# Two MLPs behind retention attention: layer 2's first product of two groups as seven half-depth products, with the decay mask made on the chip, eight more load buffers and idle matmuls at the start

## The chip, the cores and the metric

The kernel runs on one core of a Trainium2 chip. The metric is the device time of one execution in microseconds (us); shown is the median of three runs. Engines: TensorE (PE) multiplies matrices, VectorE (DVE), ScalarE (ACT) and GpSimd (POOL) work on elements, SyncE (SP) issues the DMAs, which run on the core's DMA engines.

## What is computed

Retention attention over 2 batches, 8 heads, 768 steps, head width 64; its output, as 1536 tokens of width 512, goes through two MLPs of hidden width 2048. Everything is float32.

```python
gamma = 1.0 - 2.0 ** (-5.0 - np.arange(H, dtype=np.float32))
for t in range(S):
    state = gamma[None, :, None, None] * state + np.einsum('bhd,bhe->bhde', k[:, :, t], v[:, :, t])
    y[:, :, t] = scale * np.einsum('bhd,bhde->bhe', q[:, :, t], state)
...
h = x @ w_in                      # layer 1
P = a[0] + a[1] * h + a[2] * h2 + a[3] * h3
Q = 1.0 + np.abs(b[0]) * np.abs(h) + np.abs(b[1]) * h2
x = (P / (Q + 1e-06)) @ w_out
...
h = x @ w_in                      # layer 2
y = (h * (1.0 / (1.0 + np.exp(-h)))) @ w_out
```

## The kernel before

The attention is cut into 12 chunks of 128 tokens. A chunk loads q and k transposed (`qT`, `kT`) and k and v (`kn`, `vn`), makes scores on PE (L435), multiplies them by the decay mask `msk` on DVE (`am`, L317), forms the output from the masked scores and v (L480) and from the state (L490), and grows the state (L468), which DVE keeps in `bd`. Four chunks make a group of 512 tokens; there are three groups, 0, 1 and 2.

Each MLP product is made of three matmuls on split operands: high part times high part, low times high, high times low. High parts of x lie in `xh[g]`, low ones in `xl[g]`, those of the weights in slots (`ih`, `il` for the first product, `oh`, `ol` for the second). The hidden width is cut into 16 blocks of 128, two to a pair. A step is one group and one block: 12 matmuls of 128x512 into one of the banks `h0` and `h1` (`mm_in`, L526), the activation on ACT and DVE, the split of the result into `gh` (ACT) and `gl` (DVE or POOL), and 12 matmuls into the four banks `acc0` to `acc3` (L576). A layer is 3 groups x 8 pairs x 2 steps. In layer 1 the runs of pairs are mixed between the groups so that the MLP can begin when group 0 has its four chunks; in layer 2 the groups come in the order 1, 0, 2.

Weights: `weights()` loads 512 KB in two halves per pair, converts them on ACT and DVE into `wt`, splits them on ACT (high, L386) and on POOL or DVE (low, L391), and stores `wt` to DRAM (`spill`), from where later groups load it again. There are four slots, and two more once the attention's buffers are free.

Helpers record every operation: `act` (L309), `tt` (L317), `stt` (L324), `dma` (L343, DMAs on SP). The order of all operations on all engines is one table, `ORDER`, read by `Flow.order`; the numbers in `R` are those with which the table was planned. At the start eleven idle matmuls (L644) run on PE while the first loads come in, and the mask `msk` is loaded from DRAM (512 KB).

Of the kernel before, what the change touches and what calls it, by code (L numbers as in the profile page):

```python
# [23 lines left out]
R = {'lw': -463.92, 'T0': 689.59, 'tau0': 13.93, 'tau1': 122.19, 'c0': -129.63, 'dc': 67.51, 'conv': 39.61, 'half': 427.29, 'absl': -34.77, 'raw': 455.03, 'ret': 752.06, 'spl': -417.39, 'hi': 301.24, 'lo': 31.56, 'inn': -277.93, 'later': -32.81, 'split': -554.53, 'out': 359.39, 'evac': -363.13, 'qload': -20.08, 'scl': 238.79, 'sc': 858.37, 'am': -44.15, 'gr': 112.48, 'av': -547.62, 'bd': 198.47, 'xh': -201.14, 'xl': 110.32, 'glp': 25, 'lop1': 15, 'lop2': 30, 'scp': 0, 'ps': 17, 'ksc': 103.89, 'qa': -467.29, 'ka': 4, 'late': 20, 'mid': 4, 'pev': -317.29, 'pld': -385.01, 'cg': -489.85, 'wm': 11, 'mk': 26.43, 'ck': 21.3, 'g2': (1, 0, 2), 'ch0': 269.21, 'ch1': -102.81, 'ch2': 64.3, 'ch3': 22.33, 'ch4': -52.46, 'ch5': 5.42, 'ch6': -78.23, 'ch7': 237.84, 'ch8': 90.06, 'ch9': -61.88, 'ch10': -106.39, 'ch11': -212.52, 'ru0': 218.22, 'lu0': -107.8, 'ru1': 40.68, 'lu1': -106.06, 'ru2': 91.09, 'lu2': 146.01, 'ru3': -37.17, 'lu3': -39.51, 'rhalf': 125.38}  # L24
# [11 lines left out]
    '3f9Kq7zc;LI4FTNa6Ha{=}-YHVJVD;@o*Gm!z`E`lVNg9fmtyJ=ENb85>sJntb-%5F6P3aFbD=iZp?%AurW5pCO86X;zXQ)qoF>Ig)z_!Ti_^c',
    'iIZ?NPR5xq4W{E#n2*b#F*U&PkOsSAcbo`QU;?DabeI-1U|wvF-LMso#nw0#C&6Tx3caug_Qp1t4{PB#oQC;vHWb1FSP<J{J6w)EaR&CmzSs{J',
    ';!IqC?Xf=&z*)EgS7JjPh;v{r%*Hji2v^}+oCh6n5H`YDuoHLTZd{G~a1ZXsb+{fk;6~hpi*YYDp{8^I58@&0gq?8#bj0~E1iRo|yo`tO2sWeU',
    'v=E-+Qd|s6;3{s$qj&`u!415IH*p1Qf{ic-r{HqvNUNb0^`J4h0k+_CT!!;-4IIN~cpW>@EqsNmU?sf97ucC@;~l(<ZKxLw!=X4Bx8V-lil=Zb',
    '9LJZ~noi>z>`8C2E#1TKxE=3fJL*mE@I8LO_H+V&;yU<&E$Ab5p{~@2e&HYdi|gSxKERgr2}4q73Ps^43|+v7corYwXWR@YaS5Km#k7hx(mw=3',  # L40
# [696 lines left out]
```

## Time and profile before

| | |
|---|---|
| median of three runs | 593.6 us (593.54 to 593.75) |
| the profiled execution's own time | 591.33 us |
| its span, from first to last instruction | 589.5 us |
| mean granted clock of PE | 0.997 |
| PE, DVE, ACT, POOL busy | 574.0, 417.5, 394.2, 132.9 us |

Busy time is the sum over an engine's instructions, share of the span in brackets in the rows below. The granted clock is a share of PE's full speed. A name such as `h` in the trace stands for all buffers of that name (`h0` and `h1`). The trace records a float32 matmul of the attention and of the warming twice, one of the MLP products once.

### The profile page before, as it was taken

Reading aid. Unit: us, or ns where it says so; the run is one execution under the profiler, and the core shown is the slowest. Engines: PE = TensorE matmul, PEld = TensorE weight load, DVE = VectorE, ACT = ScalarE, POOL = GpSimd, SP = SyncE. Lnnn points to the kernel's source line nnn. Section 1 sums busy time; section 2 is a strip of 40 time slices with the busy share of each in tenths; the row PEclk is TensorE's granted clock in tenths of the full one; section 3 lists DMA queues with packets and bytes.
Section 4 is the critical chain, followed back from the end, with each engine's and each line's share of the span. In section 5 each row is a group of like instructions: output and inputs, shape, how many; then the busy total and the mean of one; then the engine's idle time right before and its main releaser. Section 6 shows DMA issues by size and latency. Waiting matters only on the chain.

```text
span 589.5 us, 8100 instructions
## 1 busy us (share of the span) xinstructions
PE 574.0 (97%) x2950; PEld 474.0 (80%) x2950; DVE 417.5 (71%) x646; ACT 394.2 (67%) x690; POOL 132.9 (23%) x104
## 2 busy tenths in 40 slices
PE   6969999999999999999999999999999999999997
PEld 5858787888888888888888888878888888888885
DVE  2899999999899999999999977765332213233320
ACT  7887788999999887787999887764522312424212
POOL 0554674464435200000114364300000000000000
PEclk9998999999999999999999999999999999999999
DMA  8996855543122201302226565462320000130001
GB/s 327 339 370 239 303 192 162 180 125 117 62 81 81 73 1 36 126 18 91 76 68 214 179 212 152 156 217 84 108 89 1 1 1 18 54 123 3 0 1 72
DMA packets 33368, 70.02 MB, mean 119 GB/s; under 512 B 3632, under 2 KB 3632, under 8 KB 33328
## 3 DMA queue, kind: packets, MB, share of 16 engines
q1 hardware_dynamic: 33328, 69.51, 35.1%
q8 instruction: 23, 0.38, 0.3%
q14 instruction: 17, 0.14, 0.1%
HBM read 56.91 MB, written 12.58 MB: 118 GB/s over the span
## 4 chain that ended last, share of the span: by engine, by line
PE 91%; DMA 4%; DVE 2%; ACT 1%; issue 1%; SPq 0%; ACTq 0%
PE acc L576 43%; PE h L526 43%; DMA kT<-in_kt_dram 2%; PE a L490 2%; PE a L435 2%; PE a L480 1%; DVE wt L324 1%; DMA raw<-in_moe_w_out_dram 1%; DMA qT<-in_qt_dram 1%; PE a L468 1%; SPq L343 0%; ACT raw L309 0%; DVE am L317 0%; DVE w L324 0%; PE h L468 0%
## 5 line engine op out<-in xcount | busy, mean ns | idle before, releaser
L526 PE MATMUL h<-xh,ih 128*128 128x512 f32 x384 | 150.2, 391 | 0.1
L526 PE MATMUL h<-xh,il 128*128 128x512 f32 x384 | 149.5, 389 | 0.0
L526 PE MATMUL h<-xl,ih 128*128 128x512 f32 x384 | 149.4, 389 | 0.0
L324 DVE SCALAR_TENSOR_TENSOR w<-w,h 128x512 f32<-128x512 f32 x48 | 32.6, 684 | 78.4 <-ACT w L309 78.2
L526 PEld LDWEIGHTS h<-xh,ih 128*128 128x128 f32 x384 | 72.1, 188 | 16.1 <-DVE s L324 0.6
L526 PEld LDWEIGHTS h<-xh,il 128*128 128x128 f32 x384 | 72.1, 188 | 15.0
L526 PEld LDWEIGHTS h<-xl,ih 128*128 128x128 f32 x384 | 72.1, 188 | 14.8
L309 ACT ACTIVATE w<-h 128x512 f32<-128x512 f32 x48 | 28.1, 593 | 78.7 <-PE h L526 74.2
L576 PE MATMUL acc<-gh,oh 128*128 128x512 f32 x192 | 75.9, 395 | 0.0
L576 PE MATMUL acc<-gh,ol 128*128 128x512 f32 x192 | 74.8, 390 | 0.0
L576 PE MATMUL acc<-gl,oh 128*128 128x512 f32 x192 | 74.8, 390 | 0.0
L576 PE MATMUL acc<-oh,gh 128*128 128x512 f32 x192 | 74.7, 389 | 0.0
L576 PE MATMUL acc<-ol,gh 128*128 128x512 f32 x192 | 74.7, 389 | 0.0
L576 PE MATMUL acc<-oh,gl 128*128 128x512 f32 x192 | 74.7, 389 | 0.0
L317 DVE TENSOR_TENSOR gl<-w,gh 128x512 fp32r<-128x512 f32 x48 | 34.0, 715 | 44.1 <-ACT gh L309 44.1
L391 POOL TENSOR_TENSOR ol<-wt,oh 128x512 fp32r<-128x512 f32 x28 | 38.6, 1389 | 105.6 <-ACT oh L386 94.4
L309 ACT ACTIVATE gh<-w 128x512 fp32r<-128x512 f32 x48 | 29.8, 629 | 46.7 <-PE acc L576 31.6
L324 DVE SCALAR_TENSOR_TENSOR wt<-wt,raw 128x512 int32<-128x512 int32 x64 | 45.0, 707 | 12.0 <-ACT raw L309 7.2
L391 POOL TENSOR_TENSOR il<-wt,ih 128x512 fp32r<-128x512 f32 x28 | 39.5, 1419 | 51.3 <-ACT ih L386 34.2
L309 ACT ACTIVATE raw<-raw,par 128x512 int32<-128x512 uint32 x64 | 48.1, 758 | 1.5 <-DMA raw<-in_moe_w_in_dram 0.8
L324 DVE SCALAR_TENSOR_TENSOR s<-s,par,h 128x512 f32<-128x512 f32 x65 | 48.2, 744 | 1.0
L317 POOL TENSOR_TENSOR gl<-s,gh 128x512 fp32r<-128x512 f32 x26 | 35.2, 1353 | 59.4 <-ACT gh L309 37.7
(88 smaller groups left out, 960.2 us busy)
## 6 DMA issues: line engine op xcount, KB each, us to landing
raw<-in_moe_w_out_dram SPq DMA_DIRECT2D x32, 512.0 KB, 3.7
raw<-in_moe_w_in_dram SPq DMA_DIRECT2D x32, 512.0 KB, 4.6
spill<-wt SPq DMA_DIRECT2D x32, 256.0 KB, 4.6
wt<-spill SPq DMA_DIRECT2D x32, 256.0 KB, 3.0
qT<-in_qt_dram SPq DMA_DIRECT2D x12, 256.0 KB, 5.7
kT<-in_kt_dram SPq DMA_DIRECT2D x12, 256.0 KB, 5.7
vn<-in_v_dram SPq DMA_DIRECT2D x12, 256.0 KB, 6.0
kn<-in_k_dram SPq DMA_DIRECT2D x10, 256.0 KB, 5.6
```

The source lines that it names most:

```text
L309: lambda: nc.scalar.activation(out=out_, in_=in_, func=func, **kw),
L317: op(eng, dur, rank, lambda: e.tensor_tensor(out=out_, in0=in0, in1=in1, op=alu), reads, writes, port)
L324: lambda: nc.vector.scalar_tensor_tensor(out=out_, in0=in0, scalar=scalar, in1=in1, op0=op0, op1=op1),
L391: e.tensor_tensor(out=sl.t[nm + "l"][:, us], in0=wt.t, in1=sl.t[nm + "h"][:, us].bitcast(F32), op=ALU.subtract)
L435: nc.tensor.matmul(heads(sb_[j].t)[:, hp, :], kT.t[js, hp, :], qT.t[js, hp, :], start=True, stop=True)
L468: nc.tensor.matmul(st.t[j * D : (j + 1) * D, hp * D : (hp + 1) * D], kn.t[:, 2 * hp + j, :], vn.t[:, 2 * hp + j, :], start=(hp == 0), stop ...
L480: nc.tensor.matmul(heads(xo.t)[j * D : (j + 1) * D, hp, :], vn.t[:, 2 * hp + j, :], heads(am[j].t)[:, hp, :], start=(hp == 0), stop=not mo ...
L490: nc.tensor.matmul(heads(xo.t)[:, hp, :], old.t[:, hp, :], qT.t[:, hp, :], start=False, stop=True, skip_group_check=True,)
L526: nc.tensor.matmul(h.t, sl.t[w][:, ws], x[g].t[:, c, :], start=(n == 0), stop=(n == 3 * KD - 1))
L576: nc.tensor.matmul(a.t, a1, a2, start=(first and n == 0), stop=(last and n == 2))
```

## The change

In layer 2 the group 1 is worked as before. Then groups 0 (`ga`) and 2 (`gb`) are taken together, pair by pair from 7 down to 0 (`joint`): their first products, two groups by two blocks, are made as seven products of half the depth (L798, 6 matmuls each) of sums of weights and sums of x, and put together by five additions out of PSUM on DVE. The sums of x are made once during the stage of group 1 (`x_sums`, L689, L706) into slots 4 and 5; the sums of weights in each pair, with their high and low parts in the space of `xh[1]` and `xl[1]`. Only group 0's second products (`project`, L628) run in the joint stage; the gates of group 2 go to DRAM (`gates`, 16 of 256 KB) and come back for a last stage, which only makes second products (`remaining`). In layer 2 four slots are left for weights.

At the start the mask is no longer loaded: 256 KB of decays come in, are spread over the partitions by two float32 matmuls (L902) and made into `msk` by eight DVE operations (L912). Eight buffers for `kT` and `vn` of the chunks 2 to 5 are lent from space that is used for weights later; `vn` has two turns in place of three, `qT` four in place of three. Eleven groups of three idle matmuls (L927) stand between the first chunks' work. All scaling of k runs on POOL. The table `ORDER` is another one. Diff, cut to its core:

```diff
-            runs = [(g, range(NPR) if n % 2 == 0 else range(NPR - 1, -1, -1)) for n, g in enumerate(R["g2"])]
+            g1, ga, gb = R["g2"]
+            runs = [(g1, range(NPR)), ((ga, gb), range(NPR - 1, -1, -1)), ((gb,), range(NPR))]
...
+        if l == 1 and use_order[i - 1][0] == 0:
+            free = [r for r in free if r < RING]
+            resident = {key: r for key, r in resident.items() if r < RING}
...
-    again = {key for key, _, old in loads.values() if old}
+    again = {(key, h) for i, (key, _, old) in loads.items() if old for h in range(2) if use_order[i][1] != (gb,) or h}
+    again |= {((1, p), 0) for p in range(NPR)}
...
+    gates = [Buf(f"gate{f}", [P, GT], F32, dram) for f in range(NF)]
...
+    spare = [x for n in ("u2", "s1", "r", "t") for x in ew[n].bufs]
...
-    kns, vns = Turns("kn", 3, [P, H, D], F32, at), Turns("vn", 3, [P, H, D], F32, at)
-    qTs, kTs = Turns("qT", 3, [P, HP, P], F32, at), Turns("kT", 2, [P, HP, P], F32, at)
+    kns, vns = Turns("kn", 3, [P, H, D], F32, at), Turns("vn", 2, [P, H, D], F32, at)
+    qTs, kTs = Turns("qT", 4, [P, HP, P], F32, at), Turns("kT", 2, [P, HP, P], F32, at)
+    first_stack = ExitStack()
+    fpool = first_stack.enter_context(tc.tile_pool(name="first", bufs=1, side="right", reuse_waits="tile"))
+    lent = {
+        (n, c): Buf(f"{n}_c{c}", [P, H, D] if n in ("kn", "vn") else [P, HP, P], F32, fpool) for n, c in R["lent"]
+    }
     gqs = Turns("gq", 2, [P, HP, P], F32, at)
     ams = [Buf(f"am{j}", [P, GT], F32, at) for j in range(2)]
...
+            buf = lent.get((name, c)) or turns()
...
-        op("pe", 2.72, now - R["inn"], mm_in, win + xh[g].all + xl[g].all, [h])
+        op("pe", 2.72, now - R["inn"], mm_in, win + xh[g].all + xl[g].all, [h] + [fill] * (s == 0))
...
+    def sum_part(i, c, lo):
+        sl, n = slots[RING + i // 2], "io"[i % 2] + "hl"[lo]
+        return sl, n, slice(c * GT, (c + 1) * GT), sl.cells[n, c]
...
+        for c in range(2):
+            chain(0, c, (of(xh[gb], c), of(xh[ga], c)), ((*of(xl[gb], c), add), (*of(xl[ga], c), sub)))
+        for c in range(2):
+            t1 = full[0, c]
+            chain(1, c, (of(xh[gb], 2 + c), (lambda t1=t1: t1.t, [t1])), ((*of(xl[gb], 2 + c), add),))
+        for c in range(2):
+            t2 = full[1, c]
+            chain(3, c, (of(xh[ga], 2 + c), (lambda t2=t2: t2.t, [t2])), ((*of(xl[ga], 2 + c), add),))
+        for c in range(2):
+            chain(2, c, (of(xh[gb], 2 + c), of(xh[gb], c)), ((*of(xl[gb], 2 + c), add), (*of(xl[gb], c), sub)))
...
+    def joint(u, p, first, last):
+        now = at_step[2 * u]
+        sl = slots[slot_of_use[u]]
+        q = p % 2
+        wu = []
+        for half in range(2 if u in loads else 1):
+            for un in range(2):
+                wt = wts()
+                kept = spill[(1, p), half, un]
+                dma(now - R["ret"] + half, 0.66, wt.t, kept.t, [kept], [wt])
+                if u in loads:
+                    parted(u, 1, sl, "io"[half], un, wt, now - R["conv"] + R["half"] * half + un)
+                if half == 0:
+                    wu.append(wt)
+        (a11, a21), (a12, a22) = (
+            [wt.t[:].rearrange("p (c j f) -> p j c f", c=2, j=2)[:, j] for j in range(2)] for wt in wu
+        )
+        tmp = [temp(), temp()]
+        s1, s2, s3, s4 = (t.t[:].rearrange("p (s c f) -> p s c f", s=2, c=2)[:, i] for t in tmp for i in range(2))
+        rk = now - R["wsum"]
+        tt("dve", rk, s1, a21, a22, ALU.add, wu, [tmp[0]], n=GT // 2)
+        tt("dve", rk, s2, s1, a11, ALU.subtract, [wu[0]], [tmp[0]], n=GT // 2)
+        tt("dve", rk, s3, a11, a21, ALU.subtract, [wu[0]], [tmp[1]], n=GT // 2)
+        tt("dve", rk, s4, a12, s2, ALU.subtract, [wu[1], tmp[0]], [tmp[1]], n=GT // 2)
+        wh, wl = xh[g1], xl[g1]
+        for r in range(2):
+            k = 2 * q + r
+            act(rk, wh.t[:, k, :], tmp[r].t, AF.Copy, [tmp[r]], wh.cells[k])
+            tt("dve", rk, wl.t[:, k, :], tmp[r].t, wh.t[:, k, :].bitcast(F32), ALU.subtract, [tmp[r], *wh.cells[k]], wl.cells[k])
...
+        def product(b_, w, x, start):
+            def mms():
+                n = 0
+                for c in range(2):
+                    for wlo, xlo in ((0, 0), (0, 1), (1, 0)):
+                        nc.tensor.matmul(
+                            b_.t, w[0](c, wlo), x[0](c, xlo), start=(start and n == 0), stop=(n == 5), skip_group_check=True
+                        )
+                        n += 1
+            op("pe", 1.36, now - R["inn"], mms, w[1] + x[1], [b_])
+        n = NPR - 1 - p
+        b0_, b1_, b2_ = (bank[("a0", "a1", "h0", "h1")[(3 * n + i) % 4]] for i in range(3))
+        c12, c21, c22 = temp(), temp(), temp()
+        def plus(to, b_, x):
+            tt("dve", now, to.t, b_.t, x.t, ALU.add, [b_, x], [to], port=False)
+        product(b0_, block(0, 0), x_of(ga, 0), True)
+        act(now, c12.t, b0_.t, AF.Copy, [b0_], [c12], True)
+        product(b1_, wsum(1), xsum(1), True)
+        plus(c21, b1_, c12)
+        product(b0_, block(1, 0), x_of(ga, 1), False)
+        product(b1_, wsum(0), xsum(0), False)
+        plus(c22, b1_, c12)
+        product(b2_, wsum(2), xsum(2), True)
+        plus(c22, b2_, c22)
+        product(b1_, wsum(3), x_of(gb, 1), False)
+        plus(c12, b1_, c12)
+        product(b2_, block(1, 1), xsum(3), False)
+        plus(c21, b2_, c21)
+        for j, (h, psum_h, mine) in enumerate(((b0_, True, True), (c12, False, False), (c21, False, True), (c22, False, False))):
+            w = ew["w"]()
+            act(now, w.t, h.t, AF.Tanh, [h], [w], psum_h, scale=0.5)
+            to = w if psum_h else h
+            stt(now, to.t, w.t, 1.0, h.t, ALU.add, ALU.mult, [w, h], [to], port=not psum_h)
+            j = j // 2
+            if mine:
+                second(now, ga, sl, j, to, first and j == 0, last and j == 1)
+            else:
+                dma(now + R["spl"], 0.66, gates[2 * p + j].t, to.t, [to], [gates[2 * p + j]])
+    def second(now, g, sl, j, gv_, first, last):
+        gh, gl = ghs(), gls()
+        act(now + R["split"], gh.t, gv_.t, AF.Copy, [gv_], [gh])
+        tt("dve", now + R["split"], gl.t, gv_.t, gh.t.bitcast(F32), ALU.subtract, [gv_, gh], [gl])
+        project(now, 1, g, sl, j, gh, gl, first, last, None)
+    def remaining(u, p, first, last):
+        sl = slots[slot_of_use[u]]
+        for j in range(2):
+            now = at_step[2 * u + j]
+            gv_ = temp()
+            dma(now - R["ret"], 0.66, gv_.t, gates[2 * p + j].t, [gates[2 * p + j]], [gv_])
+            second(now, gb, sl, j, gv_, first and j == 0, last and j == 1)
...
-    warm = ew["u2"].bufs[0]
+    warm = Buf("warm", [P, P])
...
+    shared[1] = gqs()
+    dma(R["mk"], 0.66, shared[1].t[:].rearrange("p a x -> p (a x)"), decays[0], [], [shared[1]])
+    pick, ones = ew["s1"].bufs[0], ew["s1"].bufs[1]
...
+    for j in range(2):
+        b_ = bank[f"acc{2 + j}"]
+        def spread(j=j, b_=b_):
+            nc.tensor.matmul(
+                b_.t, pick.t[:, j * P : (j + 1) * P], shared[1].t[:].rearrange("p a x -> p (a x)"), start=True, stop=True
+            )
+        op("pe", 0.88, R["mk"], spread, [pick, shared[1]], [b_])
+        for a in range(HP):
+            op(
+                "dve",
+                0.27,
+                R["mk"],
+                lambda j=j, a=a, b_=b_: nc.vector.scalar_tensor_tensor(
+                    out=msk.t[:, j, a, :],
+                    in0=heads(b_.t)[:, a, :],
+                    scalar=gk[:, 1, 2 * a + j : 2 * a + j + 1],
+                    in1=ones.t[:, 0:P],
+                    op0=ALU.mult,
+                    op1=ALU.mult,
+                ),
+                [b_, cst, ones],
+                [mcs[j]],
+            )
...
+    def filling():
+        for _ in range(3):
+            nc.tensor.matmul(bank["h0"].t[:, 2 * P : 3 * P], warm.t[:, 0:P], warm.t[:, 0:P], start=True, stop=True)
+    for n in range(R["fill"]):
+        op("pe", 0.65, R["fl"] + 1.5 * n, filling, [warm], [fill])
...
-        if u in loads:
+        if u in loads and g != (ga, gb):
             weights(u)
+        if l == 1 and use_order[u - 1][0] == 0:
+            x_sums(at_step[2 * u + 6])
         opens = u == 0 or use_order[u - 1][:2] != (l, g)
         closes = u == n_use - 1 or use_order[u + 1][:2] != (l, g)
         part = "out" if l == g == 0 and u < NPR else "in" if l == g == 0 else None
+        if g == (ga, gb):
+            joint(u, p, opens, closes)
+            s += 2
+            continue
+        if g == (gb,):
+            remaining(u, p, opens, closes)
+            s += 2
+            continue
         for n, j in enumerate((0, 1) if p % 2 == 0 else (1, 0)):
             step(s, l, g, u, j, opens and n == 0, closes and n == 1, part)
             s += 1
...
```

PE at the very start, before (`a0`, `a1`, `acc0`, `h1` are banks; L435 makes scores, L480 outputs):

```order
L644 MATMUL h1_156<-u2_0_132 128x128 x11
L435 MATMUL a0_149<-qT_0_168,kT_0_171 128x128
L435 MATMUL a1_150<-qT_0_168,kT_0_171 128x128
...
L435 MATMUL acc0_151<-qT_1_169,kT_1_172 128x128
L435 MATMUL acc1_152<-qT_1_169,kT_1_172 128x128
...
L480 MATMUL h1_156<-am0_175,vn_0_165 64x128
L480 MATMUL h1_156<-am1_176,vn_0_165 64x128
```

and now (L867 is the warming, L902 the spreading, L927 idle matmuls, L474 scores):

```order
L867 MATMUL h1_186<-warm_218 128x128 x11
L902 MATMUL acc3_184<-gq_0_214,s1_0_166 128x512
L902 MATMUL acc2_183<-gq_0_214,s1_0_166 128x512
L927 MATMUL h0_185<-warm_218 128x128 x6
L474 MATMUL a0_179<-qT_0_197,kT_0_201 128x128
L474 MATMUL a1_180<-qT_0_197,kT_0_201 128x128
...
L927 MATMUL h0_185<-warm_218 128x128 x6
L474 MATMUL acc2_183<-qT_2_199,kT_c2_206 128x128
L474 MATMUL acc3_184<-qT_2_199,kT_c2_206 128x128
```

Two spreading matmuls and six idle ones stand ahead of the first scores, six more ahead of the second chunk's.

DVE in layer 2 about where the joint stage begins: before, only gates (L324) and their low parts (L317):

```order
L324 SCALAR_TENSOR_TENSOR w_1_135<-w_1_135,h1_156 128x512
L317 TENSOR_TENSOR gl_1_147<-w_0_134,gh_1_144 128x512
L317 TENSOR_TENSOR gl_2_148<-w_1_135,gh_2_145 128x512
L324 SCALAR_TENSOR_TENSOR w_0_134<-w_0_134,h0_155 128x512
L317 TENSOR_TENSOR gl_0_146<-w_0_134,gh_0_143 128x512
```

and now the additions out of the banks `a0`, `a1`, `h0` (L350), weight sums of 256 columns, low parts of sums into `xl1` and `il5`, and gates (L357):

```order
L350 TENSOR_TENSOR xl1_69<-u2_0_162,xh1_68 128x512
L689 TENSOR_TENSOR il5_1683<-t_0_171,ih5_1682 128x512
L350 TENSOR_TENSOR s1_1_167<-a1_180,u2_1_163 128x512
L350 TENSOR_TENSOR u2_0_162<-wt_4_161,wt_0_157 128x256
L350 TENSOR_TENSOR s1_1_167<-h0_185,s1_1_167 128x512
L350 TENSOR_TENSOR t_0_171<-a0_179,r_1_170 128x512
L350 TENSOR_TENSOR u2_0_162<-u2_0_162,wt_4_161 128x256
L350 TENSOR_TENSOR u2_1_163<-a1_180,u2_1_163 128x512
L350 TENSOR_TENSOR xl1_69<-u2_0_162,xh1_68 128x512
L357 SCALAR_TENSOR_TENSOR u2_1_163<-w_1_165,u2_1_163 128x512
L350 TENSOR_TENSOR s1_0_166<-h0_185,s1_0_166 128x512
L350 TENSOR_TENSOR t_1_172<-a0_179,r_1_170 128x512
```

The sums of the next pairs' weights and the additions of the pairs under way share the engine.

SP late in layer 2: before, reloads of weights and stores of the output:

```order
L343 DMA wt_4_131<-spill1601_113 128x512
L343 DMA wt_2_129<-spill1011_107 128x512
L343 DMA wt_3_130<-spill1600_112 128x512
L343 DMA wt_2_129<-spill1700_116 128x512
L621 DMA out_0_dram<-t_0_141 128x512
```

and now, at the end of the joint stage, gates going out and coming back:

```order
L376 DMA wt_1_158<-spill1510_124 128x512
L376 DMA gate2_136<-s1_2_168 128x512
L376 DMA gate1_135<-s1_0_166 128x512
L376 DMA gate0_134<-u2_0_162 128x512
L376 DMA s1_0_166<-gate8_142 128x512
L376 DMA s1_2_168<-gate1_135 128x512
L376 DMA s1_1_167<-gate0_134 128x512
L376 DMA gate3_137<-r_1_170 128x512
L376 DMA wt_3_160<-spill1610_128 128x512
L376 DMA r_0_169<-gate2_136 128x512
```

A gate's load stands right behind the stores of the last gates.

## Rows read from the trace of the kernel before

**Rows 1.** The page, parts 1 and 4: busy time, chain that ended last

```profile
PE 574.0 (97%) x2950; PEld 474.0 (80%) x2950; DVE 417.5 (71%) x646; ACT 394.2 (67%) x690; POOL 132.9 (23%) x104
...
PE 91%; DMA 4%; DVE 2%; ACT 1%; issue 1%; SPq 0%; ACTq 0%
PE acc L576 43%; PE h L526 43%; DMA kT<-in_kt_dram 2%; PE a L490 2%; PE a L435 2%; PE a L480 1%; DVE wt L324 1%; DMA raw<-in_moe_w_out_dram 1%; DMA qT<-in_qt_dram 1%; PE a L468 1%; SPq L343 0%; ACT raw L309 0%; DVE am L317 0%; DVE w L324 0%; PE h L468 0%
```

**Rows 2.** Busy time by stage; columns stand in the first line

```profile
core 0: us, PE busy (x) PEld busy (x) DVE busy (x) ACT busy (x) POOL busy (x), PEclk, DMA share, GB/s
6.48:27.58 21.10, 15.76 (x248) 14.25 (x248) 14.74 (x25) 18.15 (x50) 7.80 (x6) 1.00 1.02 365
...
34.10:47.65 13.55, 9.12 (x113) 7.97 (x113) 12.27 (x20) 10.67 (x18) 8.78 (x7) 0.87 0.97 345
...
126.70:328.00 201.30, 201.30 (x889) 166.26 (x889) 195.63 (x301) 177.47 (x298) 49.13 (x36) 1.00 0.26 83
...
415.00:502.00 87.00, 87.00 (x386) 72.06 (x384) 25.05 (x39) 24.31 (x43) 0.00 (x0) 1.00 0.12 37
502.00:589.50 87.50, 83.35 (x368) 68.72 (x366) 24.80 (x38) 25.86 (x46) 0.00 (x0) 1.00 0.12 43
```

**Rows 3.** The chain in layer 2, from 440: start us, us, what

```profile
439.83 2.72 PE acc L576 x12
442.55 2.72 PE h L526 x12
```

**Rows 4.** Timeline of PE, 0 to 28: start, us, what, idle before, releaser

```profile
1.45 5.03 PE L644 MATMUL h<-u 128*128 128x128 f32 x22 [1.45 <-DVE par L648]
...
21.45 1.16 PE L435 MATMUL a<-qT,kT 64*128 64x128 f32 x16 [0.82 <-DMA qT<-in_qt_dram]
22.54 0.69 PE L468 MATMUL h<-vn,kn 128*64 128x64 f32 x16
23.06 0.28 PE L480 MATMUL h<-u,vn 128*64 128x128 f32 x1
...
24.03 1.16 PE L490 MATMUL h<-qT,bd 128*128 128x128 f32 x8
25.12 0.69 PE L468 MATMUL h<-vn,kn 128*64 128x64 f32 x16
```

**Rows 5.** Timeline of PE, 34 to 48

```profile
36.66 1.09 PE L480 MATMUL a<-am,vn 128*64 128x128 f32 x16 [1.39 <-DVE am L317]
...
41.01 1.16 PE L435 MATMUL a<-qT,kT 64*128 64x128 f32 x16 [1.56 <-DVE bd L317]
43.66 0.98 PE L468 MATMUL a<-vn,kn 128*64 128x64 f32 x16 [1.49 <-DVE am L317]
44.42 1.92 PE L480 MATMUL a<-am,vn 128*64 128x128 f32 x16
46.28 1.62 PE L490 MATMUL a<-qT,bd 128*128 128x128 f32 x8
47.65 0.48 PE L526 MATMUL h<-xh,ih 128*128 128x512 f32 x1
```

**Rows 6.** Timeline of DVE at the start

```profile
9.62 1.29 DVE L317 TENSOR_TENSOR am<-a,msk 128x512 f32<-128x512 f32 x2 [8.21 <-DMA msk<-in_consts_dram]
...
23.37 0.42 DVE L317 TENSOR_TENSOR bd<-h,bd 64x256 f32<-64x256 f32 x1
```

**Rows 7.** Timeline of DVE in layer 2

```profile
440.49 1.29 DVE L324 SCALAR_TENSOR_TENSOR w<-w,h 128x512 f32<-128x512 f32 x2 [3.50 <-ACT w L309]
442.48 0.69 DVE L317 TENSOR_TENSOR gl<-w,gh 128x512 fp32r<-128x512 f32 x1 [0.70 <-ACT gh L309]
```

**Rows 8.** Timeline of ACT in layer 2

```profile
441.81 0.63 ACT L309 ACTIVATE gh<-w 128x512 fp32r<-128x512 f32 x1 [1.35 <-DVE w L324]
```

**Rows 9.** DMA issues from 384 on: KB each, median us to landing

```profile
wt<-spill SPq DMA_DIRECT2D x16, 256.0 KB, 3.3
spill<-wt SPq DMA_DIRECT2D x8, 256.0 KB, 3.6
```

**Rows 10.** A stretch of the start by windows, columns as in rows 2

```profile
43.40:46.80 3.40, 3.14 (x34) 2.81 (x35) 3.36 (x6) 1.85 (x4) 1.98 (x2) 0.57 1.02 386
```

More of the change, by code (lines that the diff above doesn't have):

```diff
@@ L36 @@
[L36 to L40, printed above, removed]
@@ L256, in __init__, with make @@
             self.chunk = [[r[o] for r in self.cells] for o in range(CPG)]
+        def make(self, pool=cpool):
+            self.t = pool.tile([P, KD, GT], F32R, tag=self.name, name=self.name)
     xh = [Parted(f"xh{g}") for g in range(NG)]
     xl = [Parted(f"xl{g}") for g in range(NG)]
+    for g in range(NG - 1):
+        xh[g].make()
+        xl[g].make()
     class Slot:
@@ L352, in weights @@
         for half in range(2):
+            if half == 0 and use_order[u][1] == (gb,):
+                continue
             w = w_dram[l][half].bitcast(I32)
@@ L448, in attention @@
                 ALU.mult,
-                [sb_[j], msk],
+                [sb_[j], mcs[j]],
                 [am[j]],
@@ L455, in attention @@
         if more:
-            gq = shared[ci] if ci in shared else load(0.5, gqs, decays[ci - 1])
-            shared[ci] = gq
+            if ci not in shared:
+                shared[ci] = load(0.5, gqs, decays[ci - 1])
+            gq = shared[ci]
             eng = "dve" if c < R["scp"] else "pool"
@@ L558, in step, with project @@
         tt("pool" if s <= R["glp"] else "dve", now + R["split"], gl.t, gv_.t, gh.t.bitcast(F32), ALU.subtract, [gv_, gh], [gl])
+        project(now, l, g, sl, j, gh, gl, first, last, part)
+    def project(now, l, g, sl, j, gh, gl, first, last, part):
         for m in range(4):
@@ L624, in step, with lazy, rows @@
                 )
-    dma(R["mk"], 1.32, msk.t[:].rearrange("p j a t -> p (j a t)"), consts[:, NGAM:], [], [msk])
+    def lazy(eng, rank, out_, in0, in1, alu, reads, writes, n=GT, port=True):
+        e = {"dve": nc.vector, "pool": nc.gpsimd}[eng]
+        dur = 0.07 + n / 960.0 if eng == "dve" else n / 418.0
+        op(eng, dur, rank, lambda: e.tensor_tensor(out=out_(), in0=in0(), in1=in1(), op=alu), reads, writes, port)
+    def rows(x, k):
+        return lambda: x.t[:, k, :].bitcast(F32)
@@ new lines, in sum_part, with x_sums, split, chain @@
+    def sum_part(i, c, lo):
+        sl, n = slots[RING + i // 2], "io"[i % 2] + "hl"[lo]
+        return sl, n, slice(c * GT, (c + 1) * GT), sl.cells[n, c]
+    def x_sums(rank):
+        sub, add = ALU.subtract, ALU.add
+        full = {}
+        def split(i, c, t):
+            sh_, nh, cs, ch = sum_part(i, c, 0)
+            sl_, nl, cs, cl = sum_part(i, c, 1)
+            op("act", 0.52, rank, lambda: nc.scalar.activation(out=sh_.t[nh][:, cs], in_=t.t, func=AF.Copy), [t], [ch])
+            lazy(
+                "dve", rank, lambda: sl_.t[nl][:, cs], lambda: t.t, lambda: sh_.t[nh][:, cs].bitcast(F32), sub, [t, ch], [cl]
+            )
+        def chain(i, c, first, terms):
+            t = temp()
+            full[i, c] = t
+            (f0, r0), (f1, r1) = first
+            lazy("dve", rank, lambda: t.t, f0, f1, sub, r0 + r1, [t])
+            for f, r, alu in terms:
+                lazy("dve", rank, lambda: t.t, lambda: t.t, f, alu, r, [t])
+            split(i, c, t)
+        def of(x, k):
+            return rows(x, k), x.cells[k]
+        for c in range(2):
[8 more added lines that the diff above has]
+            chain(2, c, (of(xh[gb], 2 + c), of(xh[gb], c)), ((*of(xl[gb], 2 + c), add), (*of(xl[gb], c), sub)))
```

195 lines of the change are left out of this document (131 added, 64 removed).

## The prediction

> **What bounds the kernel now.** I read the page's busy line and its chain first [rows 1]: TensorE (PE) is busy 97% of the span, 91% of the chain that ended last is PE, and the two lines of the MLP products, L526 and L576, hold 43% each. The reader should see that VectorE (DVE, 71%) and ScalarE (ACT, 67%) do not set the total. An average hides stages, so the windows come next [rows 2]: from 126.70 to 328 and from 415 to 502 PE is busy every microsecond (201.30 of 201.30, 87.00 of 87.00). Its only idle time before the tail lies at the start: 21.10 - 15.76 = 5.3 us up to 27.58 and 13.55 - 9.12 = 4.4 us up to 47.65. So a change pays in two ways: by fewer matmuls anywhere, or by filling these early gaps. The chain in layer 2 [rows 3] gives the price of a matmul: twelve of L526 follow each other in 2.72 us, twelve of L576 too, 0.227 us each, with nothing between. Last I read PE's own timeline of the start [rows 4, 5], where each wait stands in brackets with what ended it.
>
> **Term A, the products.** In layer 2 a pair of hidden blocks cost groups 0 and 2 two steps of twelve L526 matmuls each, 48. The change makes seven half-depth products of six matmuls (L798), 42. Six fewer in eight pairs are 48 fewer, of one shape: 48 x 0.227 = **-10.9 us**. The second products (L576, now L628) stay at 384. Because PE has no idle time there [rows 2], this is gained in full unless a new wait takes its place.
>
> **Term B, the start.** Removed: a 512 KB load (msk). In exchange the change loads 256 KB of decays first and spreads them with two fp32 matmuls of 128x512. It lends eight buffers so that chunks 2 to 5 load early, runs chunks 0 to 4 to the end before the first MLP step, and adds 33 idle matmuls in groups of three.
> - A chunk costs on PE: scores 22.54 - 21.45 = 1.09, state growth 0.52, local outputs 0.97, outputs of the state 1.09, together 3.67 us [rows 4]. Five chunks without what chunks at a sequence's head skip: 5 x 1.09 + 5 x 0.97 + 3 x 1.09 + 5 x 0.52 = 16.2.
> - An idle matmul: the trace records every fp32 matmul twice. The eleven of L644 (x22) took 5.03 us, 0.46 each; four of the same shape at L490 took 25.12 - 24.03 = 1.09, 0.27 each with the start of their group [rows 4]. I take 0.23, since they follow others without such a start: 33 x 0.23 = 7.6 us. The ends are 7.1 and 15.1. The two spreading matmuls have four times the columns: about 2.0 together.
> - Walk: the warming ends near 6.2, + 2.0 + 7.6 + 16.2 = 32.0. Two steps of 2.72 end at 37.5. Chunk 5 with its mask wait (3.7 + 1.4, [rows 5]) ends at 42.6. The third step needs bank h0, which DVE should release near 43.0. With chunk 6, which stood ahead of it before (3.7), this point is reached at 46.7, where the kernel before stands at 47.65 [rows 5]: **-0.9 us**. Loads don't hold it: the queues move 365 GB/s [rows 2], 0.72 us per 256 KB, and the last load for chunk 4 is about the 32nd such piece, in by 27.
> - The bounds: -4 if the idle matmuls all lie inside the waits that remain, +3 if they all lie on the path. Of the DVE rows, the mask used to come by DMA and the first masked product waited 8.21 us for it [rows 6]. Eight small multiplications now make it, a 64x256 one costs 0.42 [rows 6], so some 3 us from the spreading on: ready near 11, where it is first asked for near 12. The cover is thin, and if it goes the wait is under 1 us.
>
> **Term C, the joint stage.** Per pair PE runs 42 + 24 matmuls, 66 x 0.227 = 15.0 us. DVE runs four half-width sums, two low halves of them, five additions out of PSUM, four multiplications for the gates and two low halves of gates: 4 x 0.42 [rows 6] + 13 x 0.65 = 10.1 us (two rows of layer 2 together take 1.29, [rows 7]), 12.7 where weights are converted too. ACT runs 9 to 13 of some 0.63 [rows 8], 8 us at most. Neither is the bound by its sum. A product that adds onto a bank must wait for the addition that reads that bank, but the order mostly puts one or two products (1.36 each) or second products between. At the start ten products stand in a row with none of layer 2's second products between, while DVE still has the sums of the pairs 7, 6 and 5 to make: I walked DVE's rows there and find one wait of some **+1.3 us** for the low half of pair 5's weight sums. Bounds: 0, and 3.
>
> **Term D, the gates that go out and come back.** The last gates of group 2 are added, passed through tanh, multiplied, stored (3.6), loaded (3.3, [rows 9]) and split. With 0.6 to 0.7 for each of five steps beside it and the issues' own time, 13.7 us, against 63 matmuls between, 14.3 us. I take **+0.5 us** for the join. The other fourteen have more room. SP's queue gets 62 more rows, but moves 37 to 43 GB/s in these stages [rows 2], a tenth of what it moved at the start. In the first stage of layer 2 DVE gets 36 more sums, some 130 rows in 90 us, 1.4 per us, under the 301 in 201.30 us of layer 1 [rows 2], where PE never waited: 0.
>
> **Sum.** -10.9 - 0.9 + 1.3 + 0.5 = -10.0. The profiled execution took 591.3 us, so 581.3 by its clock. The median of the runs is 593.6, 2.3 above it, and I carry that over: **583.6 us**.
>
> **The clock.** In the stretch from 43.40 to 46.80 the granted clock was 0.57 of full speed [rows 10], close to the lower of the levels 1.2 and 2.4 GHz, after waits of 1.39, 1.56 and 1.49 us [rows 5]; chunk 6's outputs took 1.92 and 1.62 there, [rows 5] where 0.97 and 1.09 are usual [rows 4]. The idle matmuls may keep such a stretch away, and 1.5 us with it, which is part of the bound of -4 in term B. The Trainium skill, "TensorE: Matmul & The Clock Gate", section "Part 1: The HAM clock gate", says that the throttled state is the default and that activity releases it. By that rule these rows are as they should be, and term B would come out nearer to -2.4 than to -0.9.
>
> **Rivals.**
> - A, the start pays in full and the joint stage doesn't wait: -10.9 - 4.0 - 0.5 = -15.4, **578.2 us**. For it: 9.7 us of idle time to fill [rows 2]. Against: PE's work there grows by 9.6 us.
> - B, the start loses: idle matmuls at 0.3 instead of 0.23, or DVE, 12.27 of 13.55 us busy [rows 2], a step behind: **587.5 us** (+3 in place of -0.9).
> - C, **slower**: the joint stage is bound by the round trip product, addition, product. Five additions per pair wait on PE and PE on them. If each is exposed at 0.69 [rows 7], it is 8 x 3.45 = 27.6 us; half of it exposed, 13.8, gives **597.4 us**. It decides from 10.0 / 8 = 1.25 us per pair above my walk. Against: second products stand between after pair 5. For: kernel before never needs such a turn, as its banks h0 and h1 alternate, and a wait for ACT between a product and its gate (3.50, [rows 7]) is hidden only by that.
> - D, PE's short waits in the joint stage pull the clock to its lower level, as they did at 43.40: four such stretches of 3.4 us at 0.57 [rows 10] cost 1.5 each, +6, **589.6 us**. The Trainium skill, same page, section "A second HAM failure mode: psum-queue depth-cycling", tells of just this: short idle times of PE between groups of matmuls that cycle through the banks, and a clock that swings between its levels. No stretch of layer 2 in the trace before shows it, since PE doesn't pause there.
> - E, the change doesn't do what it says: the stored gates return late because their loads stand in SP's queue behind stores that wait for DVE. At 1.2 us for each of the eight last pairs, 9.6: **593.2 us**.
>
> **How the numbers follow.** Forecast 0.53 (its own range 580 to 587), A 0.17, B 0.14, C 0.08, D 0.05, E 0.03. What a measurement of this kernel can tell from no change is about 0.2%, 1.2 us. Faster by more: the forecast, A, B and D, 0.89, less a little for B's and D's upper tails, 0.88. Within: E and the lowest of C, 0.04. Slower: C, 0.08. The range leaves out C, E and a little of A's lower end: 577.5 to 590.0.
>
> **What would show it.** Right: L798 with 336 matmuls of 0.227 apart, and a joint stage that lasts about 8 x 15.0 + 1.3 = 121 us with PE busy 99%; the wait of about 1 us near its start, for DVE's low half (line 350); the third step of L575 near 43; no wait for a gate over 0.5 us. Wrong: a sum of PE's waits in the joint stage above 5 us, for DVE's additions; a granted clock under 1.00 there; the third step later than 46; or a DMA behind PE's wait at the last stage.

## The result and the profile after

The changed kernel takes 586.83 us (median of four, 586.64 to 589.0), the kernel before 593.57 (median of four, 590.82 to 593.75): a ratio of 0.990, 95% interval 0.987 to 0.993, so 6.7 us less. The two profiled executions are nearer to each other: their spans are 584.7 and 589.5, 4.8 us apart. Executions of the kernel before spread with their mean granted clock (in the last comparison below its spans run from 587.7 at a mean clock of 1.000 to 594.3 at 0.987), those of the changed kernel all have 1.000, and the profiled one of before, at 0.997, is among its shorter ones.

The page of the changed kernel, parts 1 and 4, beside [rows 1]:

```profile
PE 575.3 (98%) x2972; PEld 471.9 (81%) x2972; DVE 491.0 (84%) x794; ACT 408.6 (70%) x697; POOL 120.3 (21%) x97
...
PE 79%; DVE 8%; DMA 6%; ACT 4%; issue 2%; SPq 0%; ACTq 0%; DVEq 0%
```

TensorE is busier than before (575.3 against 574.0 us), though 48 matmuls are gone: the idle ones and the two spreading ones took their place. Its share of the chain fell from 91% to 79%, and VectorE and DMAs now hold 14% of it. Its waits in the whole execution (engine, line, what was waited for: us in total, times, longest):

```profile
PE a L520 <- DVE am L350: 1.4, 1, 1.4
PE h L575 <- DVE s L357: 1.2, 1, 1.2
PE h L867 <- DVE warm L863: 1.1, 1, 1.1
PE h L927 <- ACT bd L342: 0.9, 1, 0.9
PE a L508 <- POOL kn L350: 0.4, 1, 0.4
PE acc L628 <- DVE gl L350: 0.2, 1, 0.2
PE h L520 <- DVE xl L557: 0.2, 1, 0.2
```

All but one of them lie before 48 us. The stages, in the columns of [rows 2]:

```profile
0.00:47.65 47.65, 42.41 (x439) 36.09 (x440) 35.04 (x65) 26.95 (x48) 22.91 (x24) 1.00 0.91 314
...
126.70:328.00 201.30, 201.30 (x920) 164.60 (x919) 193.14 (x300) 170.50 (x285) 39.86 (x30) 1.00 0.24 78
...
400.00:526.00 126.00, 125.77 (x552) 103.21 (x551) 102.40 (x180) 59.23 (x107) 0.00 (x0) 1.00 0.31 105
```

The joint stage (400 to 526, with the end of group 1 at its start) is full: 125.77 of 126. The chain inside it:

```profile
441.77 1.36 PE h L798 x6
443.13 1.36 PE a L798 x6
444.49 2.72 PE h L798 x12
447.21 2.04 PE acc L628 x9
```

Six matmuls of L798 in 1.36 us, 0.227 each, back to back with one another and with the second products, as L526 and L576 were [rows 3]. The timeline of TensorE at the start, beside [rows 4, 5]:

```profile
1.12 4.53 PE L867 MATMUL h<-warm 128*128 128x128 f32 x22 [1.12 <-DVE warm L863]
5.48 1.88 PE L902 MATMUL acc<-gq,s 128*128 128x512 f32 x4
7.20 1.50 PE L927 MATMUL h<-warm 128*128 128x128 f32 x12
8.63 1.16 PE L474 MATMUL a<-qT,kT 64*128 64x128 f32 x16
...
13.38 0.94 PE L927 MATMUL h<-warm 128*128 128x128 f32 x6
14.24 0.69 PE L508 MATMUL h<-vn,kn 128*64 128x64 f32 x16
15.85 0.94 PE L927 MATMUL h<-warm 128*128 128x128 f32 x6 [0.93 <-ACT bd L342]
...
34.40 0.50 PE L575 MATMUL h<-xh,ih 128*128 128x512 f32 x1
...
42.62 1.09 PE L520 MATMUL a<-am,vn_c 128*64 128x128 f32 x16 [1.39 <-DVE am L350]
...
45.22 0.69 PE L508 MATMUL a<-vn_c,kn 128*64 128x64 f32 x16 [0.42 <-POOL kn L350]
47.09 0.47 PE L575 MATMUL h<-xh,ih 128*128 128x512 f32 x1 [1.18 <-DVE s L357]
```

The idle matmuls take 1.43 us for six (7.20 to 8.63; the other six take 1.53) and 0.86 for three (13.38 to 14.24); two groups of six and seven of three make 9.0 us, 0.27 each. The first step begins at 34.40 and the third at 47.09, with chunk 6 still to come; the kernel before had chunk 6 behind it when it came to its third step at 47.65 [rows 5].

**Where the time went.** I compared when TensorE starts its n-th matmul of the MLPs in either trace. Up to about the 1500th the work is the same, so that the difference is what the start and the first stages cost:

| matmul | before, us | changed, us | difference |
|---|---|---|---|
| 1 | 27.58 | 34.40 | +6.82 |
| 601 | 198.30 | 201.75 | +3.45 |
| 1153 | 323.65 | 328.91 | +5.25 |
| 1501 | 402.95 | 408.24 | +5.29 |
| end of the span | 589.5 | 584.7 | -4.8 |

So the start lost 3.4 us, another 1.8 go between the 601st and the 1153rd, where TensorE never waits (201.30 of 201.30 above), and then 10.9 us come back with some 0.8 lost again.

The 1.8 us are neither a wait nor the clock. A piece of the chain near 255, changed kernel, where TensorE works on group 2:

```profile
255.58 2.81 PE h L575 x12
```

Twelve matmuls take 2.81 us, 234 ns each, where L526 needs 2.72, 227 each [rows 3]. Matched with the program's order, only those that read `xh2` or `xl2` as their moving operand are slow (192 of L575, 48 of L798, on average 234 to 235 ns); the first products of the other groups stay near 227. The second products that stand between the slow ones lose a little too: from the 601st to the 1153rd they average 228.7 ns, in the kernel before 226.9. What the change did to these two buffers: they now lie on the right side of SBUF, in the space lent to `kT` and `vn` at the start.

### The profile page after: what moved, and what is told of

Same layout as the page of the kernel before. It is cut to its first block, busy times and chain, and to the rows that moved or that the text cites. A ratio compares the mean times of both kernels' runs of the same rounds, so it can differ in the third digit from the quotient of the medians.

```text
span 584.7 us, 8423 instructions
## 1 busy us (share of the span) xinstructions
PE 575.3 (98%) x2972; PEld 471.9 (81%) x2972; DVE 491.0 (84%) x794; ACT 408.6 (70%) x697; POOL 120.3 (21%) x97
## 4 chain that ended last, share of the span: by engine, by line
PE 79%; DVE 8%; DMA 6%; ACT 4%; issue 2%; SPq 0%; ACTq 0%; DVEq 0%
PE acc L628 36%; PE h L575 22%; PE h L798 7%; PE a L798 6%; DMA raw<-in_moe_w_in_dram 4%; DVE wt L357 3%; DMA spill<-wt 2%; PE a L474 2%; PE h L927 1%; PE a L530 1%; PE a L520 1%; ACT raw L342 1%; DVE gl L350 1%; ACT wt L342 1%; PE h L867 1%
## 5 line engine op out<-in xcount | busy, mean ns | idle before, releaser
L575 PE MATMUL h<-xh,ih 128*128 128x512 f32 x256 | 100.7, 393 | 1.2 <-DVE s L357 1.2
L575 PE MATMUL h<-xl,ih 128*128 128x512 f32 x256 | 100.2, 391 | 0.0
L575 PE MATMUL h<-xh,il 128*128 128x512 f32 x256 | 100.1, 391 | 0.0
L628 PE MATMUL acc<-gh,oh 128*128 128x512 f32 x192 | 75.8, 395 | 0.0
L628 PE MATMUL acc<-oh,gl 128*128 128x512 f32 x192 | 75.0, 391 | 0.3 <-DVE gl L350 0.2
L628 PE MATMUL acc<-gh,ol 128*128 128x512 f32 x192 | 75.1, 391 | 0.0
L628 PE MATMUL acc<-gl,oh 128*128 128x512 f32 x192 | 74.8, 390 | 0.0
L628 PE MATMUL acc<-ol,gh 128*128 128x512 f32 x192 | 74.8, 389 | 0.0
L628 PE MATMUL acc<-oh,gh 128*128 128x512 f32 x192 | 74.7, 389 | 0.0
L575 PEld LDWEIGHTS h<-xh,ih 128*128 128x128 f32 x256 | 48.1, 188 | 12.0 <-ACT h L342 1.3
L575 PEld LDWEIGHTS h<-xh,il 128*128 128x128 f32 x256 | 48.1, 188 | 10.5
L575 PEld LDWEIGHTS h<-xl,ih 128*128 128x128 f32 x256 | 48.1, 188 | 10.1
L357 DVE SCALAR_TENSOR_TENSOR wt<-wt,raw 128x512 int32<-128x512 int32 x64 | 48.0, 754 | 6.1 <-ACT wt L342 3.3
L357 DVE SCALAR_TENSOR_TENSOR s<-s,par,h 128x512 f32<-128x512 f32 x66 | 49.1, 745 | 1.1
L342 ACT ACTIVATE wt<-raw 128x512 f32<-128x512 f32 x64 | 42.5, 668 | 7.7 <-DMA raw<-in_moe_w_in_dram 5.1
L357 DVE SCALAR_TENSOR_TENSOR wt<-raw,wt 128x512 int32<-128x512 int32 x64 | 45.1, 709 | 1.0
L342 ACT ACTIVATE s<-h,par 128x512 f32<-128x512 f32 x48 | 37.0, 774 | 9.1 <-PE h L575 5.0
L628 PEld LDWEIGHTS acc<-oh,gl 128*128 128x128 f32 x192 | 36.0, 188 | 8.7 <-DVE gl L350 1.2
L628 PEld LDWEIGHTS acc<-gh,oh 128*128 128x128 f32 x192 | 36.0, 188 | 8.1
```

The costliest lines, as they stand in the source:

```text
L342: lambda: nc.scalar.activation(out=out_, in_=in_, func=func, **kw),
L357: lambda: nc.vector.scalar_tensor_tensor(out=out_, in0=in0, scalar=scalar, in1=in1, op0=op0, op1=op1),
L575: nc.tensor.matmul(h.t, sl.t[w][:, ws], x[g].t[:, c, :], start=(n == 0), stop=(n == 3 * KD - 1))
L628: nc.tensor.matmul(a.t, a1, a2, start=(first and n == 0), stop=(last and n == 2))
```

## The experiments

**Operand starts.** The four runs of this part ask why these matmuls are slow. The remainders given here come from the compiled programs, no profile shows them: all operands of the MLP matmuls start at remainder 384 of 512 bytes, but for `xh2` and `xl2` of the changed kernel: 480.

e1: 32 bytes spare on the right side.

```diff
+    rpool = ctx.enter_context(tc.tile_pool(name="rpad", bufs=1, side="right"))
+    rpad = Buf("rpad", [P, 8], F32, rpool)
     first_stack = ExitStack()
```

> The changed kernel with a spare buffer of 32 bytes a partition allocated first on the right side of SBUF, so that the operands xh2 and xl2 start at a multiple of 64 bytes instead of 32 bytes past one; nothing else differs. Theory 'start address': in the changed kernel each 128x512 matmul that reads xh2 or xl2 as its moving operand takes about 234 ns instead of 227 (192 of L575, 48 of L798); they go back to 227 and the time falls by some 1.8 us. Rival 'place': the right side of SBUF, or other traffic at that time, makes them slow; then they stay at 234 and the time stays.

Measured: 588.08 us (586.72 to 589.2), ratio to before 0.992 (0.989 to 0.995). Matmuls that read `xh2` took 231 ns on average, those that read `xl2` 228: better, not 227. A multiple of 64 isn't what counts, and the time shows no gain.

e3: the kernel before with `xh` and `xl` shifted inside larger buffers.

```diff
-            self.t = cpool.tile([P, KD, GT], F32R, tag=name, name=name)
+            raw_ = cpool.tile([P, KD * GT + 16], F32R, tag=name, name=name)
+            o_ = {"xh0": 1, "xl0": 4, "xh1": 8, "xl1": 12, "xh2": 0, "xl2": 2}[name]
+            self.t = raw_[:, o_ : o_ + KD * GT].rearrange("p (k t) -> p k t", k=KD)
```

> The kernel before the change with the operands xh and xl moved inside larger buffers: xh0 starts 4 bytes past a multiple of 64, xl0 16, xh1 32, xl1 48, xh2 0, xl2 8. Nothing else differs. Theory 'start address': L526 matmuls that read xh1 take 234 ns instead of 227, and those of the other moved ones as well or not, which says what distance counts; if all moved ones are slow, 896 matmuls of 7 ns cost 6.5 us. Rival 'place': all stay at 227 and the time is that of the kernel before.

Measured: 598.52 us in one execution, a span of 596.7 against 589.5. Its chain:

```profile
250.24 5.59 PE h L528 x24
```

233 ns each. All L526 matmuls (L528 here) were slow, 236 for `xh0` and 232 to 233 for the others, `xh2` too, which had not been shifted in its buffer. Each larger buffer moves all that follow it by 64 bytes, so `xh2` started at remainder 0 and the weights at 256. The second products, whose weights and moving operands moved equally far, stayed at 227 to 229 on average, so the weights' new start alone isn't the cause. The run also brings the slowness into the kernel before, without the right side.

e5: 96 bytes spare (`[P, 24]` in e1's diff), which gives `xh2` and `xl2` the weights' remainder, 384. e8: the kernel before with 32 bytes spare ahead of all buffers, so that all remainders shift together.

> The changed kernel with a spare buffer of 96 bytes a partition ahead of the right side of SBUF, so that xh2 and xl2 start at the same remainder of 512 bytes as the weights that are multiplied with them (384). Theory 'same remainder': a 128x512 matmul is slowed when its moving operand and the weight block read beside it start at different remainders of 512 bytes (480 against 384 in the changed kernel, 448 with 32 bytes spare); here matmuls that read xh2 or xl2 take 227 ns and the time falls by some 2 us against the changed kernel. Rival 'place': the right side of SBUF is slower whatever the start; they stay at 230 to 234.

> The kernel before the change with a spare buffer of 32 bytes a partition ahead of all others, so that every buffer starts 32 bytes past a multiple of 64 and all keep their distances. Theory 'same remainder' (it is the difference of the two operands' starts that counts): matmuls stay at 227 ns and the time is that of the kernel before. Rival 'start address' (each operand's own start counts): L526 and L576 take 232 to 236 and the time rises by 10 us or more.

Measured, e5: 585.09 us (584.43 to 586.02), ratio 0.986 (0.980 to 0.992). Matmuls on `xh2` and `xl2` are back at 227 and 226 ns; the chain near 255:

```profile
254.96 2.72 PE h L577 x12
```

At the 1153rd matmul it stands at +3.23 instead of +5.25. e8: span 589.7 (591.55 us in one execution), and all matmuls at 227:

```profile
249.86 4.31 PE h L527 x19
```

So it is the difference of the two operands' starts. With equal remainders of 512 bytes there is no loss; with differences of 64, 96 and 256 there is. How large it is doesn't follow from the difference alone: at 64 bytes `xh2` loses 4 ns and `xl2` 1. The Trainium skill, "SBUF — State Buffer", section "Who interferes with whom", counts two independent read ports for TensorE, one for the moving operand and one for weights, and says that it never waits on anyone. By that the starts of the two should not matter to each other; here they make 234 or 227 ns. Why they do, no run shows.

**The joint stage.** e4 makes the first product of a pair twice; e6 makes each addition twice.

```diff
-        product(b0_, block(0, 0), x_of(ga, 0), True)
+        product(b0_, block(0, 0), x_of(ga, 0), True, 2)
```

> The changed kernel with the first of the seven products of each pair made twice (the second time overwrites the first), which puts 48 matmuls of 128x512 back into the joint stage. Theory 'TensorE bounds the joint stage': it costs 48 x 0.227 = 10.9 us. Rival 'the additions bound it': the extra matmuls fall into waits and cost under 5 us.

Measured in one execution: span 595.6 (597.69 us), 10.9 above the changed kernel's, with the stage full:

```profile
400.00:537.00 137.00, 137.00 (x603) 112.86 (x602) 103.38 (x181) 60.59 (x109) 0.00 (x0) 1.00 0.30 98
```

Of the 10.9 us, 0.6 were there before the stage (the 1501st matmul starts at 408.81 in place of 408.24), so the 48 matmuls cost 10.3 where they stand. The price of term A holds to about half a microsecond, in the place where it was to be gained.

```diff
+                for r in range(2):
+                    half = slice(r * GT // 2, (r + 1) * GT // 2)
+                    nc.vector.tensor_tensor(out=dump.t, in0=b_.t[:, half], in1=x.t[:, half], op=ALU.add)
                 nc.vector.tensor_tensor(out=to.t, in0=b_.t, in1=x.t, op=ALU.add)
```

> The changed kernel with each of the five additions out of PSUM of a pair done twice on VectorE (first as two halves into a spare buffer), 0.7 us more per addition, 28 us in all. Theory 'TensorE bounds the joint stage, with slack between product and addition': much of it is covered, the joint stage of 126 us grows by under 10 us. Rival 'the round trip bounds it': every addition lies between two products and the stage grows by over 20 us.

Measured in one execution: span 605.8 (607.48 us), 21.1 more. From the first product of the first pair to the last of the last pair it takes 144.1 us in place of 125.5, 18.6 more; another 3.2 come behind it, most of them at the join. That is near the rival's number and far above the theory's. TensorE's longest waits from 400 to 550 are of products for additions (L815), and one at the join for a gate's high half:

```profile
PE a L799 <- DVE t L815: 2.6, 2, 1.4
PE a L799 <- DVE u L815: 2.1, 2, 1.9
PE h L799 <- DVE s L815: 2.0, 3, 1.3
PE acc L629 <- ACT gh L343: 1.9, 1, 1.9
PE a L799 <- DVE s L815: 1.4, 3, 0.7
```

VectorE's busy time from 400 on rose by 30.7 us (122.8 to 153.5). About 9 of them were covered, 1.1 us a pair. That is all the slack of the stage and the join (of VectorE's time and of the turn from product to product, which this run does not tell apart), so rival C was not far off, though as it stands no product waits.

**The start.** e2 takes the idle matmuls away (`range(0)` in place of `range(3)` in `filling`).

> The changed kernel without the 33 idle matmuls (L927); the order of everything else is the same. Theory 'on the path': their 9.0 us lie mostly on the path of the start; the first step of layer 1 begins some 6 us earlier than 34.4 and the whole falls by 4 to 6 us, what remains going into waits for weights, for the mask and for the copies of the state. Rival 'cover': they stand in waits that come back in full and the clock falls to its lower level in some stretch; the time stays within 1 us or rises.

Measured: 586.02 us (584.31 to 587.83), ratio 0.989 (0.985 to 0.993). Waits and the stretch up to the first step:

```profile
PE h L520 <- DVE xl L557: 2.5, 2, 1.6
PE acc L474 <- DVE msk L912: 2.0, 1, 2.0
PE acc L628 <- DVE gl L350: 1.8, 2, 1.3
```

```profile
5.60:30.90 25.30, 20.69 (x272) 17.27 (x271) 21.15 (x37) 13.04 (x25) 14.74 (x13) 0.93 1.02 358
```

Both theories have a part. The first step comes 3.6 us earlier (30.83) and the third as well (43.51), of 9.0 that were taken out: the rest comes back as waits for `xl` and the mask, and the mean granted clock falls to 0.93 there, with one stretch at its lower level (0.51 from 12.40 to 15.80). But the 3.0 us that TensorE is ahead at the 601st matmul are 1.1 at the 1501st, and it waited near 338 and again near 416, both times for `gl`, low halves of gates made on VectorE. In the median the rival has it: 0.8 us less than the changed kernel, with ranges that overlap.

**VectorE between 330 and 420.** e7, e9, e10 and e11 try to keep these us by moving work to GpSimd: e7 all 28 sums of x (`"dve"` to `"pool"` in `x_sums`), e9 and e10 eight low halves of weights (`lop2` 28 to 30), e11 sixteen (`lop2` 32); e9 keeps the idle matmuls, the others don't; all have e5's spare.

> The changed kernel with three mends: no idle matmuls, xh2 and xl2 at the weights' remainder of 512 bytes, and the 28 operations that make the sums of x on GpSimd (idle from 330 on) in place of VectorE. Theory 'VectorE takes the start's gain back at the join': without the idle matmuls alone TensorE came 3 us earlier out of the start and lost it in waits for VectorE at 338 and 415; with the sums off VectorE those near 415 go, and the whole falls by 3 to 6 us against the changed kernel. Rival: GpSimd, at 1.4 us an operation in place of 0.7, delivers the sums late, or its operations slow those of VectorE beside them; then the joint stage waits at its start and the time stays or rises.

> The changed kernel with xh2 and xl2 at the weights' remainder of 512 bytes, and the low halves of two more pairs' weights of layer 2 (8 operations of L429) on GpSimd in place of VectorE; the idle matmuls stay. Theory 'VectorE is the limit from 330 to 415': with the remainder alone TensorE was 2.0 us ahead of the changed kernel at its 1152nd matmul of the MLPs and only 0.2 at the 1500th; with 8 x 0.6 = 4.8 us less on VectorE it keeps the 2.0, and the whole is 1 to 2 us under the 584.0 of span measured with the remainder alone. Rival: GpSimd makes VectorE's operations beside it slower, as when it had the 28 sums of x; then nothing is gained or TensorE waits for gl.

> The same without the 33 idle matmuls of the start. Theory 'VectorE is the limit from 330 to 415': the start gives 3 us and these are kept, span near 580. Rival: VectorE has too little room even so; span 583 to 586 with waits for gl between 330 and 420.

> The same with all low halves of the weights that are new in the stage of group 1 on GpSimd (16 operations moved in place of 8). Theory: as before or up to 1 us better, span 579 to 580. Rival: GpSimd's 16 x 1.4 us more make the weights late; TensorE waits for ol or il near 395 to 410 and the span is over 583.

Measured: e7 596.13 us (594.46 to 598.88, ratio 1.005, 1.002 to 1.008), e9 588.04 (585.69 to 588.68), e10 585.38 (582.85 to 586.75), e11 588.46 (586.68 to 590.61). e10 is the best of them and no better than e2 or e5 within their spread; the rivals have it. In e7, whose granted clock was also lower (0.95 from 330 to 400, 0.97 from 420 to 470):

```profile
PE acc L630 <- DVE gl L352: 4.8, 4, 2.3
PE a L800 <- POOL ol L691: 2.9, 1, 2.9
```

Why is shown by GpSimd's and VectorE's rows in e9's timeline:

```profile
338.25 1.29 POOL L431 TENSOR_TENSOR il<-wt,ih 128x512 fp32r<-128x512 f32 x1 [2.42 <-ACT ih L426]
338.30 1.80 DVE L352 TENSOR_TENSOR gl<-w,gh 128x512 fp32r<-128x512 f32 x1
```

VectorE's operation on two operands in SBUF, which started 0.05 us after GpSimd's, lasts 1.80 us, not 0.69: it ends 0.56 after GpSimd's. This is no single case: in the changed kernel from 100 us on, 21 such operations of 128x512 started inside one of GpSimd's, and each ended 0.55 to 0.69 us after it. Another 59 that started so had an operand in PSUM, and they lasted 0.67 to 0.75 all the same. One of each, the first with an operand in the bank `h`:

```profile
104.39 1.30 POOL L350 TENSOR_TENSOR gl<-s,gh 128x512 fp32r<-128x512 f32 x1 [5.64 <-ACT gh L342]
104.69 0.67 DVE L350 TENSOR_TENSOR s<-s,h 128x512 f32<-128x512 f32 x1
...
106.91 1.30 POOL L429 TENSOR_TENSOR il<-wt,ih 128x512 fp32r<-128x512 f32 x1 [0.22 <-ACT ih L424]
107.77 0.99 DVE L357 SCALAR_TENSOR_TENSOR wt<-wt,raw 128x512 int32<-128x512 int32 x1
```

From 330 to 420 the changed kernel has 3 such long rows (over 0.85 us), e2 and e5 have 5, e9 12, e11 18, e7 20, with 9 to 27 operations on GpSimd; what the long rows last above 0.76 us sums to 1.8, 3.5, 9.4, 14.9 and 16.7 us, in the same order. Moving eight operations of 0.6 us saved 4.8 and cost 6 to 8. The Trainium skill, "SBUF — State Buffer", section "Who interferes with whom", says this: GpSimd shares a port pair with VectorE, and of a GpSimd instruction that reads SBUF and a VectorE one with two inputs there, the second waits for the first to end. These rows agree.

e12 joins the two mends that cost VectorE nothing: no idle matmuls, and e5's spare.

> The changed kernel without the idle matmuls and with xh2 and xl2 at the weights' remainder of 512 bytes, all else as it is (the low halves and the sums stay on VectorE). Theory: at the 1152nd matmul of the MLPs TensorE is 3 + 2 = 5 us ahead of the changed kernel, and VectorE takes 3 to 4 of them back between 330 and 420, where its rows are full; 1 to 2 us remain, median 584.5 to 586. Rival: the two gains add up, median 582; or the start without idle matmuls ends in a clock at its lower level more often and the runs spread to 588.

Measured: **583.53 us** (581.09 to 584.82, six executions), ratio 0.985 (0.981 to 0.988), the best of all: 10 us under the kernel before, and 3.3 under the changed one's own median. Its profiled execution, the shortest, has a span of 579.0 and no wait between 330 and 420:

```profile
330.00:420.00 90.00, 90.00 (x398) 74.17 (x397) 82.88 (x134) 68.10 (x120) 13.09 (x10) 1.00 0.68 222
```

It had 3 long rows, like the changed kernel. I had expected VectorE to take a part of the gain back; in this execution it didn't. The median stands between theory and rival. What makes three collisions of one execution five in another was not tried.

## Why the prediction was right, and where it was not

The direction, the range and the largest term held. But 583.6 was 3.2 us too low, and that it was no further off is luck: on the profiled execution the forecast was -10.0, to 581.3, and that took 586.83, 4.5 less than before.

- **Term A, -10.9: right.** 288 of the 336 matmuls of L798 take 0.227 us, and 48 put back cost 10.3.
- **Term B, -0.9: the step that failed.** It came to +3.4 (at the 601st matmul), beyond its own bound of +3. One of its signs of being wrong came, too: the third step later than 46. That step was due at 43.0 and came at 47.09, 4.1 late, in two parts. The first step began at 34.40 in place of 32.0, for the most part because the 33 idle matmuls took 9.0 us, not 7.6 (0.27 each, which L490 had shown [rows 4], but I had put it down to the start of a group), and because of a wait of 0.93. And I let bank h0 come free near 43.0 whatever the idle matmuls do. But the step that fills h0 comes first, and VectorE's chain that frees the bank moves with it: from the first step to the third it took 12.69 us here and 12.68 in e2, where both came 3.6 us earlier; I had 11.0. Rival B had named that, and the price of +3 it gave is about what was measured. That its total, 587.5, was nearer than the forecast is in part luck: it holds terms C and D, which did not come, in place of the next item.
- **Not foreseen: +1.8 and some tenths** for the remainder of `xh2` and `xl2`. The diff shows that they are made late, on another side; nothing in the trace before could give the price, as all starts agree there.
- **Term C, +1.3, and D, +0.5: too high.** No product waits over 0.1 us for an addition or for a low half of a weight sum, and no second product at the join for a gate; the one wait from 400 us on is 0.2, for gl, at the end of group 1. Rival C decided from 1.25 us a pair of exposed turns; none was exposed, and by e6 about 1.1 us a pair were still to spare.
- **The 2.3 us carried over from the profiled execution to the median: wrong.** In the comparisons of the experiments the longer executions of the kernel before have, by and large, the lower mean clocks (down to 0.986), and the profiled one, at 0.997, was among the shorter. The changed kernel keeps 1.000, and its median is its profiled time. So nothing was to be carried over, and the 2.3 hid a part of what term B was too low by.
- **The clock.** The stretch of 0.57 at 43.40 [rows 10] is gone, as the Trainium skill's rule, that activity releases the throttled state ("TensorE: Matmul & The Clock Gate", section "Part 1: The HAM clock gate"), would have it. That rule's result for term B, -2.4, was further off than mine: without the idle matmuls, and with a stretch at the lower level, e2 was 3.0 us ahead at the 601st matmul. Rival D did not come: 1.00 in the whole joint stage.
- **A slip in rival A.** Its sum takes 0.5 off for term D, which the forecast had added; without waits in the joint stage it would be 578.7, not 578.2.

## What to carry to other kernels

Price each matmul that is put in to fill gaps at its full length, and move with it whatever is released at the end of the chain behind it; a bank's release is not a fixed time. When a buffer moves to another place, compare the starts of the operands that TensorE reads side by side, by their remainder of 512 bytes, and count the matmuls that read it. Before work goes from VectorE to an idle GpSimd, count VectorE's operations with two SBUF operands beside it; each that meets one of GpSimd's may cost more than the one moved.
